# Scores of a gated linear attention by halves of the sequence chunk, in quarters of the TensorE array

## The chip, the cores and the metric

The kernel runs on one core of a Trainium2 chip. The metric is device time in microseconds for one execution, as the median of several runs. Its engines are TensorE (PE in the profile; its weight loads are shown as PEld), VectorE (DVE), ScalarE (ACT), GpSimd (POOL) and SyncE (SP), which only issues transfers here.

## The reference

Two blocks, one after the other. The first is a recurrence per head, with 4 batches, 8 heads, 768 steps and a head size of 48:

```python
state = alpha[:, :, t, :, None] * state + np.einsum('bhd,bhe->bhde', k[:, :, t], v[:, :, t])
y[:, :, t] = np.einsum('bhd,bhde->bhe', q[:, :, t], state)
```

The second takes y as x, 3072 tokens by 384 features (a token's eight heads side by side):

```python
h = x @ w_in            # 384 -> 2048
g = h - np.tanh(h)
return g @ w_out        # 2048 -> 384
```

All is float32.

## The kernel before

**Units and chunks.** A batch's 768 steps are cut into three units of 256 steps (TU), so there are 12 units, numbered u = 0 to 11; a unit has two chunks of 128 steps (c = 0, 1). Inside a chunk the recurrence is a masked product: with U and W, the running products of alpha from both ends (two scans on VectorE, L684 and L700), k is multiplied by U and q by W. Then *scores* (L757) form, for every head, a matrix over s (the step of k and v, 128 partitions) and t (the step of q, 128 columns). *masked* (L767) multiplies it by a triangle, so that s <= t alone is left, on its way from PSUM to the tile pm in SBUF. *products* (L795 and L807) form y: the old state times q, plus v times the masked scores. *back*, *natural* and *update* (L829, L833, L842) carry k times v into the state; *features* (L824) copies y to xT, and *moves* (L885) shifts the rows of the last two heads into gaps by six small transfers, so that the 384 features fill three tiles of 128.

**Heads on the array.** Head size 48 fills less than half of the 128 rows. Heads lie in pairs: four groups g, each with two heads, r = 0 on partitions 0 to 47 and r = 1 on 64 to 111. `head(g, r)` (L527) says which head that is. The two score matmuls of a group use the two row halves of the array; each has 128 weight columns (the steps s) and streams 128 columns (the steps t). Scores of r = 0 and r = 1 lie in one PSUM bank each. The product with the old state (L795) has 48 rows and 64 weight columns, that is one quarter of the array.

**The feed-forward part.** Each unit has eight steps s of `moe` (here a step is 256 of the 2048 features): a first product of 12 matmuls of 128x256 (L951), squares and other functions on ScalarE, products on VectorE (L968, L972, L984 to L986), and a second product, eight matmuls of 128x384 in units 0 and 1 (L996), fourteen of 128x192 from unit 2 on (L1011).

**What sets the order.** All of it is written as tasks (`add`, `go`, `go_c`): a name, an engine, an assumed time in us, a rank, the tasks it comes after, and a function that issues it. `Planner` simulates the engines with these assumed times, in eight rounds with different priorities, and takes the order with the earliest end. The instructions are then issued in that order, and each engine works through its own in order. Waits between engines come from the tiles they share. Transfers are issued on SyncE's queue, all but a few at the start: loads of alpha, k, q (four per unit and tensor, L587), of v (two per unit, L569), weights (L43), moves and stores. v of unit u is loaded once y of unit u - 2 is done, since its buffer has two places.

**Where k, q and alpha come from.** From unit 2 on (and alpha of unit 1) they land as rows of eight steps, get widened on ScalarE (L617) and transposed in 32x32 blocks on VectorE (`flip`, L622). For units 0 and 1 (`TURNED`) they go through TensorE (`turn`, L639).

**PSUM.** The pool ps_sc has two banks, sc0 and sc1. Scores use both; from unit 2 on so do y, and `back` uses sc0.

Of the kernel before, what the change touches and what calls it, by code (L numbers as in the profile page):

```python
# [9 lines left out]
FP32 = mybir.dt.float32  # L10
# [411 lines left out]
def fast(tc, q, k, v, alpha, moe_w_in, moe_w_out, out, w_in, w_out, ident, ok, pad_rows):  # L422
# [17 lines left out]
    with ExitStack() as ctx:  # L440
# [21 lines left out]
        TURNED = ((0, 1, 2), (1, 2))  # L462

        def by_matmul(u, what):
            return u < len(TURNED) and what in TURNED[u]
# [4 lines left out]
        for what in TURNED[0]:  # L470
# [5 lines left out]

        mask = consts.tile([P, P], FP32, name="mask")
        GP.memset(mask, 1.0)
        GP.affine_select(out=mask, in_=mask, compare_op=ALU.is_ge, fill=0.0, base=0,
                         pattern=[[1, P]], channel_multiplier=-1)  # L480

# [37 lines left out]
        def gait(u):  # L519
            return 2  # L520

        plan = Planner()
        add = plan.add
# [3 lines left out]
        def head(g, r):  # L527

            return 2 * g + (r + g) % 2

# [29 lines left out]
        def load(u, what):  # L562

            b, i = divmod(u, UPB)
            t0 = i * TU
            if what == 3:
                vt = vts[u] = two.tile([P, CU, H, D], FP32, name="vt")
                for c in range(CU):
                    (A if u == 0 and c else nc.sync).dma_start(out=vt[:, c],  # L569
                                    in_=v[b, :, t0 + c * P:t0 + (c + 1) * P, :].rearrange("h p d -> p h d"))  # L570
                return
            t, x = raws[what], (alpha, k, q)[what]
            if by_matmul(u, what):
                if u > 0:
                    make_rough(u, what)
                to = rough[u, what][:, 0:BOTH].rearrange("p (h n) -> p h n", h=H)
                of = x[b, :, t0:t0 + TU, :].rearrange("h (p two) d -> p h (two d)", two=CU)

                for n in range(2):
                    at = slice(n * NP, (n + 1) * NP)  # L580
                    (A if u == 0 and n else nc.sync).dma_start(out=to[:, at], in_=of[:, at])  # L581
                return
            for r in range(2):
                a, z = head(0, r), head(1, r)
                src = x[b].rearrange("(e m) s d -> e m (s d)", m=4)[:, a:z + 1:z - a, t0 * D:(t0 + TU) * D]
                for m in range(2):
                    nc.sync.dma_start(out=t[HP * r:HP * r + 32, m::2].rearrange("p e t d -> p e (t d)"),  # L587
                                      in_=src[:, m].rearrange("e (i n) -> i e n", i=32))

        def gla(u, rank):  # L590
# [28 lines left out]
            def flip(what, make):  # L619
                t = make()  # L620
                for g in range(NP):
                    V.transpose(t[:, g].rearrange("p c (i r) -> p r c i", r=R), raws[what][:, g, :, 0:32])  # L622

# [5 lines left out]
            def turn(what, n):  # L629

                if u == 0:
                    pool, tag = ((ps_sc, f"sc{n}"), (ps_o, f"o{n}"), (ps_h, "h"))[what]
                else:
                    pool, tag = ((ps_sc, f"sc{n}"), (ps_o, f"o{2 + n}"), (ps_sc, f"sc{n}"))[what]
                t = m["turned", what, n] = pool.tile([P, NP, P], FP32, name="turned", tag=tag)
                for g in range(NP):
                    for r in range(2):
                        at = (head(g, r) * CU + n) * D
                        T.matmul(t[HP * r:HP * r + HP, g, :], lhsT=rough[u, what][:, at:at + HP], rhs=ident,  # L639
                                 start=True, stop=True)  # L640
# [62 lines left out]
            def scale(name, by):  # L703
                t = m[name].rearrange("p g c t -> p (g c) t")
                V.tensor_mul(t, t, m[by][:, :, 1:])

# [13 lines left out]
            if not by_matmul(u, 1):  # L720
                go("kU", "DVE", 1.2, 3, ["kT", "U"], lambda: scale("kT", "U"))
            if not by_matmul(u, 2):
# [3 lines left out]

            def bank(n, c):


                if u < PLAIN:  # L730
                    return ps_o.tile([P, NP, P], FP32, name="y", tag=f"o{n if c is None else 2 + n}")
                return ps_sc.tile([P, NP, P], FP32, name="y", tag=f"sc{n}")

            def chunk(c):
# [11 lines left out]
                def scores():  # L746
                    if c == 0:

                        xT[u] = two.tile([P, NP, TU], FP32, name="xT")
                    if u == 0 and c == 1:  # L750
                        sc = m["sc", c] = [ps_h.tile([P, 2, TU], FP32, name="h").rearrange(
                            "p a t -> p (a t)").rearrange("p (g t) -> p g t", t=P) for _ in range(2)]
                    else:
                        sc = m["sc", c] = [ps_sc.tile([P, NP, P], FP32, name=f"sc{hh}") for hh in range(2)]
                    for g in range(NP):
                        for r, q in enumerate(quads):
                            T.matmul(sc[r][:, g, :], lhsT=m["kT"][q, g, c, :], rhs=m["qT"][q, g, c, :],  # L757
                                     start=True, stop=True)

                def masked():  # L760
                    if u == 0 and c == 1:
                        pm = [two.tile([P, NP, P], FP32, name=f"pm{hh}", tag=tag) for hh, tag in enumerate("zw")]
                    else:
                        pm = [two.tile([P, NP, P], FP32, name=f"pm{hh}", bufs=1) for hh in range(2)]
                    m["pm", c] = pm
                    for hh in range(2):
                        V.tensor_mul(pm[hh], m["sc", c][hh], mask.unsqueeze(1).to_broadcast([P, NP, P]))  # L767

# [11 lines left out]
                def products():  # L780

                    if n == 0 and direct:
                        one = bank(0, c)
                        m["y", c] = [one, one]
                        y = [one[:, j, :] for j in range(NP)]
                    else:
                        m["y", c] = [bank(x, None if direct else c) for x in range(2)]
                        y = [m["y", c][g % 2][:, g // 2, :] for g in range(NP)]
                    pairs = [(g, r, head(g, r) % 2) for g in range(KT if direct else NP) for r in range(2)]
                    to_gap = [(j, r, hh, slice(HP * hh + D - gap, HP * hh + HP))  # L790
                              for j in range(KT) for r in range(2) for hh in [head(NP - 1, r) % 2]] if direct else []
                    vt = vts[u].rearrange("p c h d -> p c (h d)")
                    if n > 0:
                        for g, r, hh in pairs:
                            T.matmul(y[g][HP * hh:HP * hh + HP], lhsT=old[quads[r], g, :], rhs=m["qT"][quads[r], g, c, :],  # L795
                                     start=(g < 2), stop=False, skip_group_check=True)
                    for j, r, hh, at in to_gap:
# [6 lines left out]
                    for g, r, hh in pairs:  # L804
# [3 lines left out]
                                 rhs=m["pm", c][r][:, g, :],  # L808
                                 start=(n == 0 and g < (1 if direct else 2)), stop=True, skip_group_check=True)

# [4 lines left out]
                def features():  # L815
                    to = slice(c * P, (c + 1) * P)
                    y = m["y", c]
                    if n == 0 and direct:
                        A.copy(xT[u][:, 0:KT, to], y[0][:, 0:KT, :])
                        return  # L820
                    for x in range(2):
                        of = range(x, KT if direct else NP, 2)
                        rows = P if direct else ROWS
                        A.copy(xT[u][0:rows, of.start:of[-1] + 1:2, to], y[x][0:rows, 0:len(of), :])  # L824

                def back():
                    tp = m["tp", c] = bank(0 if u else 1, c)
                    for g in range(NP):
# [6 lines left out]
                def update():  # L835
                    if direct:
                        m["up", c] = bank(1, c).rearrange("p g t -> p (g t)")[:, 0:NP * D]
                    up = m["up", c].rearrange("p (g d) -> p g d", d=D)
# [14 lines left out]
                if past and not (u == 0 and c == 1):  # L853
                    held = [f"masked {past}"]
                    if u > PLAIN or u == PLAIN and c:
                        held += [f"x {past}", not past_last and f"state {past}", not last and "natural"]
                go_c("scores", "PE", 1.2, 7, kU(u) + qW(u) + held, scores)
                go_c("masked", "DVE", 1.4, 8, ["scores", f"y 0.0" if u == 1 and c == 0 else past and u > 0 and f"y {past}"], masked)
                if n > 0:
# [242 lines left out]
        def gather():  # L1102
            verdict["row"] = ps_sc.tile([P, P], FP32, name="row", tag="sc0")
            T.transpose(verdict["row"][0:1, :], verdict["fine"][:, 0:1], ident)
# [74 lines left out]
```

## Time and profile before

| | |
|---|---|
| runs | 600.43, 599.98, 601.09, 597.77 us; median 600.2 |
| the profiled execution | 597.88 us |
| its span, first to last instruction | 595.8 us |
| granted TensorE clock, mean | 0.995 |
| VectorE busy | 438.0 us |
| ScalarE busy | 322.8 us |
| POOL busy | 4.0 us |
| scores, L757 (from SBUF to ps_sc) | 368 matmuls, 285 ns each as shown |
| mask, L767 | 46 instructions of 128x512, 682 ns |
| k times U, L705 | 10 instructions of 128x1024, 1207 ns |
| transposes of k, L622 | 40 of 128x256, 623 ns |
| loads of v, L569 | 192 KB each, 3.6 us from issue to landing |

Durations of matmuls overlap: each shows from its start to the end of its way through the array, and the next starts before that. The cost of a block of matmuls is read from the distance between starts. The span is less than the execution by what lies before the first instruction and after the last. Sixteen further matmuls of scores, of unit 0's second chunk, are shown with another tile's name, because they write to a pool of the feed-forward part.

### The profile page before, as it was taken

What the parts mean: (1) busy time and instruction counts of PE and PEld (TensorE: products, weight loads), DVE (VectorE), ACT (ScalarE), POOL (GpSimd) and SP (SyncE); (2) the same over time, 40 slices, a digit from 0 to 9 for tenths busy, and PEclk for the clock granted to TensorE, in tenths of its full rate; (3) what the DMA queues carried; (4) which work ended last, traced back from release to release, by engine and by line L of the source; (5) the groups of instructions that cost most, each with busy time, mean ns of one, the idle gap of its engine ahead of it and who ended that gap; (6) DMA issues with size and microseconds to landing.
All of it is one profiled execution on the core that took longest, in us unless ns stands there. A gap on an engine that the chain in (4) does not pass through costs nothing.

```text
span 595.8 us, 10679 instructions
## 1 busy us (share of the span) xinstructions
PE 579.8 (97%) x4111; PEld 508.9 (85%) x4111; DVE 438.0 (74%) x830; ACT 322.8 (54%) x585; POOL 4.0 (1%) x18
## 2 busy tenths in 40 slices
PE   8899999999999999999999999999999999999993
PEld 8677777768999998999998999899899898899993
DVE  6968799888979886985896796986796635634742
ACT  3577996448674686576484364264453433423430
POOL 2000000000000000000000000000000000000000
PEclk9999999999999999999999999999999999999997
DMA  9999862245675464452330120220100000000001
GB/s 193 204 238 239 256 125 54 54 113 105 123 144 141 112 161 84 137 133 84 103 113 28 37 57 22 60 80 17 40 6 1 28 8 2 28 8 1 26 1 33
DMA packets 60188, 50.63 MB, mean 85 GB/s; under 512 B 35264, under 2 KB 49888, under 8 KB 60128
## 3 DMA queue, kind: packets, MB, share of 16 engines
q1 hardware_dynamic: 57216, 48.88, 34.9%
q10 hardware_dynamic: 2912, 0.98, 0.8%
q8 instruction: 34, 0.56, 0.4%
q14 instruction: 26, 0.21, 0.1%
HBM read 44.04 MB, written 4.72 MB: 82 GB/s over the span
## 4 chain that ended last, share of the span: by engine, by line
PE 90%; DMA 4%; SPq 2%; DVE 1%; issue 1%; ACT 0%; ACTq 0%; DVEq 0%
PE h L951 42%; PE o L1011 31%; PE o L996 6%; PE sc L757 3%; PE y L807 3%; DMA raw<-in_moe_w_in_dram 2%; PE y L795 2%; DMA vt<-in_v_dram 2%; PE y L842 1%; SPq L43 1%; PE y L829 1%; SPq L569 0%; DVE w_in L87 0%; DMA xT<-xT 0%; ACTq L581 0%
## 5 line engine op out<-in xcount | busy, mean ns | idle before, releaser
L951 PE MATMUL h<-xT,w_in 128*128 128x256 f32 x1152 | 266.1, 381 | 2.7 <-ACT xT L824 1.6
L951 PEld LDWEIGHTS h<-xT,w_in 128*128 128x128 f32 x1152 | 214.8, 190 | 32.3 <-ACT xT L824 1.8
L960 ACT ACTIVATE u<-h 128x512 f32<-128x512 f32 x96 | 57.1, 594 | 191.9 <-PE h L951 191.5
L968 DVE TENSOR_TENSOR w<-h,u 128x512 f32<-128x512 f32 x96 | 65.9, 686 | 89.2 <-ACT u L960 88.9
L1011 PE MATMUL o<-b,e 128*128 128x192 f32 x480 | 91.1, 326 | 0.0
L1011 PE MATMUL o<-w_out,e 128*128 128x192 f32 x320 | 81.2, 336 | 0.0
L1011 PEld LDWEIGHTS o<-b,e 128*128 128x128 f32 x480 | 80.2, 190 | 0.0
L972 DVE SCALAR_TENSOR_TENSOR g<-z,w 128x512 f32<-128x512 f32 x96 | 65.6, 684 | 14.0 <-ACT z L964 10.5
L1011 PE MATMUL o<-b,g 128*128 128x192 f32 x320 | 65.1, 326 | 0.0
L964 ACT ACTIVATE z<-u 128x512 f32<-128x512 f32 x96 | 60.3, 629 | 2.3
L1011 PEld LDWEIGHTS o<-w_out,e 128*128 128x128 f32 x320 | 55.9, 190 | 5.3 <-issue 0.5
L1011 PEld LDWEIGHTS o<-b,g 128*128 128x128 f32 x320 | 54.2, 190 | 0.0
L978 ACT ACTIVATE big<-u 128x1024 f32<-128x1024 f32 x48 | 50.2, 1046 | 0.0
L996 PE MATMUL o<-w_out,g 128*128 128x384 f32 x128 | 44.2, 489 | 0.1
L996 PEld LDWEIGHTS o<-w_out,g 128*128 128x128 f32 x128 | 24.0, 190 | 13.9 <-DVE w_out L87 0.3
L984 DVE TENSOR_TENSOR e<-g 128x256 f32<-128x256 f32 x80 | 33.3, 416 | 1.6
L985 DVE TENSOR_TENSOR e<-g 128x256 f32<-128x256 f32 x80 | 33.3, 416 | 0.0
L767 DVE TENSOR_TENSOR pm<-sc,mask 128x512 f32<-128x512 f32 x46 | 29.5, 682 | 4.9 <-PE sc L757 4.9
L757 PEld LDWEIGHTS sc<-qT,kT 48*128 48x128 f32 x368 | 22.3, 187 | 8.1 <-issue 4.5
L700 DVE TENSOR_TENSOR_SCAN W<-aT,before 128x1032 f32<-128x1032 f32 x12 | 27.6, 2300 | 0.1
L684 DVE TENSOR_TENSOR_SCAN U<-aT,after 128x1032 f32<-128x1032 f32 x12 | 27.4, 2286 | 0.1
L757 PE MATMUL sc<-qT,kT 48*128 48x128 f32 x368 | 26.7, 285 | 0.4 <-DVE rough L469 0.4
(105 smaller groups left out, 534.8 us busy)
## 6 DMA issues: line engine op xcount, KB each, us to landing
raw<-in_moe_w_out_dram SPq DMA_DIRECT2D x16, 768.0 KB, 6.9
raw<-in_moe_w_in_dram SPq DMA_DIRECT2D x32, 288.0 KB, 5.8
vt<-in_v_dram SPq DMA_DIRECT2D x23, 192.0 KB, 3.6
ar<-in_alpha_dram SPq DMA_DIRECT2D x44, 96.0 KB, 2.3
kr<-in_k_dram SPq DMA_DIRECT2D x40, 96.0 KB, 2.2
qr<-in_q_dram SPq DMA_DIRECT2D x40, 96.0 KB, 2.2
raw<-in_moe_w_in_dram SPq DMA_DIRECT2D x32, 96.0 KB, 5.9
out_dram<-same SPq DMA_DIRECT2D x20, 96.0 KB, 1.7
```

The lines of the kernel that those rows point to most:

```text
L757: T.matmul(sc[r][:, g, :], lhsT=m["kT"][q, g, c, :], rhs=m["qT"][q, g, c, :], start=True, stop=True)
L767: V.tensor_mul(pm[hh], m["sc", c][hh], mask.unsqueeze(1).to_broadcast([P, NP, P]))
L951: T.matmul(h[:, a, :], lhsT=w_in[:, j, f * P:(f + 1) * P], rhs=xT[u][:, j, :], start=(j == 0), stop=(j == KT - 1))
L960: A.activation(m["u", s], m["h", s], AF.Square, scale=W_SCALE ** -1.5)
L964: A.activation(m["z", s], m["u", s], AF.Square, bias=QB, scale=QA * W_SCALE)
L968: V.tensor_mul(m["w", s], m["h", s], m["u", s])
L972: V.scalar_tensor_tensor(out=g.rearrange("p a c t -> p (a c t)"), in0=m["z", s], scalar=QK, in1=m["w", s], op0=ALU.add, op1=ALU.mult)
L978: A.activation(big, m["us", s // 2].rearrange("p s t -> p (s t)"), AF.Relu, bias=-U_FAST, scale=W_SCALE, accum_out=over[:, n:n + 1])
L984: V.tensor_add(e[:, 0:2, :], g[:, 0], g[:, 1])
L985: V.tensor_sub(e[:, 2:4, :], g[:, :, 1, :], g[:, :, 0, :])
L996: T.matmul(m["o"][c], lhsT=g[:, a, c, :], rhs=w_out[:, f, :], start=(f == 0), stop=(f == FT - 1))
L1011: T.matmul(o[n][:, i], lhsT=g_, rhs=w_, start=(s == 0 and (n, i) in ((0, 0), (1, 0), (2, 1), (3, 0))), stop=(s == FS - 1), skip_group_chec ...
```

## The change

For units 2 to 11 (`halved`), three things go together.

*Scores.* Instead of one matmul of 128 weight columns per head, there are two of 64 weight columns. The first takes the first half of s and streams all 128 steps t; the second takes the second half of s and streams only the second half of t, since for s in the second half and t in the first the mask is zero anyway. The steps s of heads 4 to 7 (groups 2 and 3) are swapped by halves: what is the first half of s for them lies on the upper 64 partitions. So groups 0 and 2 fill the two column halves of the array at the same time, with the two heads of each in the two row halves, and matmuls are ordered by groups 0, 2, 1, 3.

*What follows from the swap.* v of heads 4 to 7 is loaded with its halves exchanged: per chunk one transfer for heads 0 to 3 and two of 64 rows for heads 4 to 7, so six per unit instead of two. The transpose of k writes groups 2 and 3 in swapped order, and its product with U becomes two instructions. The heads are placed on groups in another way (`head`), so that groups 0 and 1 hold heads 0 to 3, and the loads are grouped accordingly.

*Mask.* It is now one tile with four groups' triangles, set by three selections on GpSimd. pm is one lasting tile, whose quarters that are never written are zeroed once, at unit 2, on GpSimd. Masking is three instructions: the second half of t on all partitions for all heads, and the first half of t on 64 partitions for groups 0 and 1 and for groups 2 and 3.

Besides, for all units: scores use one tile of two banks (`two_banks`), y's groups lie in banks by g // 2 instead of g % 2, and from unit 2 on `features` is one copy of both banks instead of two. The planner's assumed times are new for three tasks of the halved units: scores 1.0 (1.2), masked 1.55 (1.4), k times U 1.4 (1.2).

```diff
+        def halved(u):
+            return u >= len(TURNED)
...
-            return 2 * g + (r + g) % 2
+            return 2 * g + (r + (g >= NP // 2)) % 2
...
+                    of = v[b, :, t0 + c * P:t0 + (c + 1) * P, :].rearrange("h p d -> p h d")
+                    if not halved(u):
+                        (A if u == 0 and c else nc.sync).dma_start(out=vt[:, c], in_=of)
+                        continue
+                    nc.sync.dma_start(out=vt[:, c, 0:NP], in_=of[:, 0:NP])
+                    for x in range(2):
+                        nc.sync.dma_start(out=vt[HP * x:HP * x + HP, c, NP:],
+                                          in_=of[HP - HP * x:P - HP * x, NP:])
...
-                    V.transpose(t[:, g].rearrange("p c (i r) -> p r c i", r=R), raws[what][:, g, :, 0:32])
+                    to = t[:, g].rearrange("p c (i r) -> p r c i", r=R)
+                    if what == 1 and halved(u) and g >= NP // 2:
+                        to = to.rearrange("p r c (x i) -> p r c x i", x=2)[:, :, :, ::-1, :]
+                    V.transpose(to, raws[what][:, g, :, 0:32])
...
+                    for half in range(2):
+                        for g in (0, 2, 1, 3):
+                            rows = HP * (half ^ (g >= NP // 2))
+                            for r, q in enumerate(quads):
+                                T.matmul(sc[r][rows:rows + HP, g, HP * half:], lhsT=m["kT"][q, g, c, rows:rows + HP],
+                                         rhs=m["qT"][q, g, c, HP * half:], start=True, stop=True)
...
+                    if u == len(TURNED) and c == 0:
+                        GP.memset(pm[HP:P, :, 0:NP // 2, 0:HP], 0.0)
+                        GP.memset(pm[0:HP, :, NP // 2:, 0:HP], 0.0)
+                    for rows, gs, ts in ((slice(0, P), slice(0, NP), slice(HP, P)), (slice(0, HP), slice(0, NP // 2), slice(0, HP)),
+                                         (slice(HP, P), slice(NP // 2, NP), slice(0, HP))):
+                        to, of = (x[rows, :, gs, ts] for x in (pm, sc))
+                        V.tensor_mul(to, of, mask[rows, gs, ts].unsqueeze(1).to_broadcast(list(to.shape)))
...
+                    if u >= PLAIN:
+                        both = m["y", c][2]
+                        A.copy(xT[u][0:ROWS, :, to].rearrange("p (a b) t -> p a b t", a=2), both[0:ROWS, :, 0:2, :])
+                        return
...
-                go_c("scores", "PE", 1.2, 7, kU(u) + qW(u) + held, scores)
+                go_c("scores", "PE", 1.0 if halved(u) else 1.2, 7, kU(u) + qW(u) + held, scores)
```

## The prediction

> **What bounds the kernel now.** I read the page's busy times first, then the chain that ended last, then TensorE's timeline inside one unit, then the queue of SyncE where a transfer stands on the chain.
>
> ```profile
> span 595.8 us, 10679 instructions
> PE 579.8 (97%) x4111; PEld 508.9 (85%) x4111; DVE 438.0 (74%) x830; ACT 322.8 (54%) x585; POOL 4.0 (1%) x18
> PE 90%; DMA 4%; SPq 2%; DVE 1%; issue 1%; ACT 0%; ACTq 0%; DVEq 0%
> ```
>
> TensorE is busy 97% of the span and is 90% of the chain. A busy PE need not be at its peak, so I looked for gaps: from 150 to 500 us the sums by stretch give PE busy all of every stretch, and DVE 79.2 of 100 us between 200 and 300. There, what TensorE no longer has to do comes off the time, while VectorE and ScalarE have room. Before 150 us it is otherwise (VectorE 26.8 of 30 us from 120 to 150).
>
> The timeline of TensorE and of its weight loads in one unit (start, length, engine, line):
>
> ```profile
> 280.81 1.16 PE L757 MATMUL sc<-qT,kT 48*128 48x128 f32 x16
> 286.97 0.67 PE L795 MATMUL y<-qT,state 48*64 48x128 f32 x16
> 288.48 0.62 PE L842 MATMUL y<-vt,kn 128*48 128x48 f32 x16
> ```
> ```profile
> 280.81 0.97 PEld L757 LDWEIGHTS sc<-qT,kT 48*128 48x128 f32 x16 [0.33 <-ACT big L978]
> 281.90 0.30 PEld L1011 LDWEIGHTS o<-w_out,e 128*128 128x128 f32 x2
> ```
>
> A block of work costs TensorE the distance from its first weight load to the next block's. Scores (L757) take 281.90 - 280.81 = **1.09 us** per chunk. Line 795 has the shape that the changed scores take, 48 rows by 64 weight columns, 128 columns streamed: 16 matmuls in 287.56 - 286.97 = 0.59 us.
>
> **The sum, part by part.**
>
> *Scores of heads by halves.* Followed one instruction at a time, the old block runs in pairs (two row halves of the array): the second pair starts 213 ns after the first, each further one 112 ns later, and the next block's load 200 ns after the last start: 213 + 6 x 112 + 7 + 200 = 1092 ns. Line 795 runs four at a time, one per quarter of the array: starts 7 ns apart within a four, the second four 160 ns after the first, further ones each 109 ns later, and 198 ns from last start to the next block. The new block has 16 matmuls of 128 columns (four fours at 109) and 16 of 64 columns (four more fours). No row shows a four of 64 columns. Nearest is line 842, where one column half loads 64 weight columns and streams 48: eight matmuls are 0.62 us less one of 0.222, over seven steps = 57 ns. Streaming 64 of 128 columns is half of 107, so also about 54 plus the same few ns. Bounds: 54 ns, if only streaming counts, to 109, if a four of half length costs as much as a full one. I take 58. Block: 160 + 3 x 109 + 4 x 58 for the starts less one step (the first short four starts at 160 + 2 x 109 + 109 = 487, the last at 661), 20 within the last four, and 54 + 91 of exit (198 less the 107 of streaming = 91) = **826 ns**. It saves 266 ns in each of 20 chunks (units 2 to 11, two each): **5.3 us**. At 109 throughout the block would be 160 + 6 x 109 + 20 + 145 = 979: 2.3 us. Units 0 and 1 keep their form.
>
> A rule speaks against the small pieces. The Trainium skill, "TensorE: Matmul & The Clock Gate", section "Wait — 56ns, not 53.3ns?", says that starts of matmuls never come closer than about 25 ns however small they are. Counted over the whole array, four would take 100 ns, and the block 160 + 3 x 109 + 3 x 100 + 75 + 145 = 1007 ns, a saving of 1.7 us in all. But the row has starts 7 ns apart in line 795, and 16 in 0.59 us with its entry and exit: the floor is not one across quarters here. I sum by the row.
>
> *The mask.*
>
> ```profile
> L767 DVE TENSOR_TENSOR pm<-sc,mask 128x512 f32<-128x512 f32 x46 | 29.5, 682 | 4.9 <-PE sc L757 4.9
> L705 DVE TENSOR_TENSOR kT<-kT,U 128x1024 f32<-128x1024 f32 x10 | 12.1, 1207 | 0.0
> L984 DVE TENSOR_TENSOR e<-g 128x256 f32<-128x256 f32 x80 | 33.3, 416 | 1.6
> L824 ACT COPY xT<-y 112x256 f32<-112x256 f32 x44 | 15.1, 370 | 16.1 <-PE y L807 12.7 <-PE y L842 2.4 <-DVE state L850 1.0
> L833 ACT COPY kn<-y 128x448 f32<-128x448 f32 x20 | 10.4, 522 | 7.5 <-PE y L829 7.4
> ```
>
> Two of 682 ns become one of 512 elements (682) and two of 256 on half the partitions (416 each, by line 984): +0.15 us x 20 = 3.0 us of VectorE. *k times U* becomes two of 512 (682): +0.16 x 10 = 1.6. The transpose into swapped halves moves as many elements; 625 ns before, I take no change (no row has this write order; double for half of the 40 would be 12.5 us of VectorE, spread over 450 us). These hide behind TensorE, which does a first product or a second product (2.2 to 2.8 us each) between scores and y. If the cover were gone, 0.15 us per chunk, 3.0 us in all, would reach TensorE. In the stage from 90 to 150 us the addition is 4 x 0.15 + 2 x 0.16 = 0.9 us against 6.3 us of VectorE's idle time.
>
> *Copies of y.* Two of 370 become one of 512 columns: 370 + (522 - 370) / 192 x 256 = 573 ns, 0.17 less, but it waits for line 842 also in its first half. x is complete about 0.2 us later; the transfers behind it stand 13 us or more ahead of their use from unit 3 on. One tile for both banks of scores adds no wait that the planner's order doesn't already have (back after x and state).
>
> *Start.* On POOL, the mask's memset grows from 128 to 512 elements (206 to about 540 ns by 428 for 384), and one selection becomes three of twice the width; ident, behind the memset, comes about 0.3 us later, the zeroed rows of the scans 1.3 us later (needed at 8.29, ready at 3.6). The 0.3 reaches the first turns on TensorE, but the chain then waits for weights of the second part (1.1 us of waiting in the products at 34.6): taken as 0, at most 0.3. Two memsets of pm on POOL at unit 2 (316 ns each by its row of 256) find POOL idle and their readers gone for 40 us: 0.
>
> *SyncE's queue.* Loads of v go from 2 transfers to 6 per unit: 40 more in all. This is the part with a price. Behind SyncE's issues stand the moves of x and the loads of alpha, k and q.
>
> ```profile
> 123.60 1.15 SPq L569 DMA_DIRECT2D vt<-in_v_dram  x2
> 124.84 3.95 SPq L885 DMA_DIRECT2D xT<-xT  x6
> 126.94 1.78 DMA xT<-xT
> 128.86 3.16 PE h L951 x12
> ```
>
> The first two lines are SyncE's timeline, the others the chain. Unit 4's v is issued just ahead of unit 2's moves, and unit 2's first product waits for the fourth move. Its waits are already 0.5 us before and 0.3 inside the product. An issue of alpha, k or q, of similar shape, takes 0.42 us with 0.05 between: six take 2.8 instead of 1.24, so the moves start **1.6 us** later, and TensorE waits that much more. Bounds: four more at 0.58 are 2.5 us; if the moves come ahead, the present 0.8 is gained. I take 1.6. Elsewhere it is hidden: unit 3's moves end at 161.7 and are used at 173.4; later units have 13 us or more; and the eight more issues at 74.7 us (v of units 2 and 3, 8 x 0.47 = 3.8 us) delay the alpha of unit 3 from a landing at about 79.6 + 2.3 = 81.9 to 85.7. Its copy on ScalarE began at 84.35, so it begins 1.3 us later. Queued behind it are a z, a sum over u and the next product's square at 88.86, which itself waited 0.37 for TensorE: it comes 0.9 late, and its reader on VectorE stands 2.2 us after its end (89.46, 91.71). So nothing of it reaches TensorE; without that gap it would be 0.9.
>
> *Sum:* -5.3 + 1.6 = **-3.7 us**. The profiled execution was 597.88 us, 2.1 outside the span; it becomes 594.2. It lies 0.4% below the median of 600.2, which becomes **596.5**. A difference under 0.5%, 3 us, can hardly be told from none here.
>
> **The rivals.**
>
> (1) *The queue costs nothing*: the planner gets new times for scores (1.0), masked and k times U, and may put the moves first. For it: it searches with these times. Against: v is ready when y is, a copy before x. 600.2 - 5.3 - 0.8 = 594.1 at best.
>
> (2) *The short fours don't pay*: a four of 64 columns takes as long as one of 128. Nothing in the profile runs it. -2.3 + 1.6 gives 599.5: no change that can be measured. Against it are the 57 ns of line 842.
>
> (3) *Slower.* The new times make another order of everything, and one queue, VectorE's in the stage of 60 to 150 us, puts the chain of a unit (scan of U, transposes, scan of W: 2.3 + 2.05 + 2.3 + 2.05 us) behind work that isn't urgent. PE then has no product ready, since unit 2 waits for its x. One such chain late, 8.7 us, gives 596.5 + 8.7 = 605.2; it decides from 3.7 + 3.0 = 6.7 us of new waits. For it: VectorE is at 88% there. Against: the added work is 0.9 us, and TensorE waits under 1 us there now.
>
> **How the numbers follow.** Forecast 0.48 (594.8 to 598.0), rival 1 0.22, rival 2 0.16, rival 3 0.14. Faster by over 0.5% (below 597.2): 0.38 of the forecast, nearly all of rival 1 (0.21), a little of rival 2 (0.01) = 0.60. Slower (above 603.2): rival 3 less its mild part, 0.11. Within: 0.29. The range 593.4 to 602.6 leaves about 0.11 of rival 3 above and 0.06 below.
>
> **What would show it.** Scores as 640 matmuls of 48 by 64, and from their first load to the next block 0.83 us (0.98: rival 2; 1.0: the floor). VectorE about 4.6 us busier, ScalarE 3.3 less. Unit 2's first product waiting for a move, with six issues of v ahead. TensorE without a gap from 150 us on. The prediction is wrong if a wait of several us appears for VectorE or SyncE before 150 us, or if the order changes how often TensorE switches its form.

## The result, and the profile after

The changed kernel takes 596.4 us in the median (41 runs), the kernel before 599.65 (62 runs). The ratio is 0.9939, with a 95% interval of 0.9925 to 0.9953, that is 3.7 us less (2.8 to 4.5). It compares means, which lie further apart than the medians, and leaves out one execution of the changed kernel (601.9 us) that fell in the chip's slower state. The forecast was 596.5, 3.7 us less than the 600.2 it started from. The number is right; two of the terms behind it are not, their errors nearly cancel, and the experiments below say which.

One pair of executions would not have shown it. The profiled execution of before, 597.88 us, is among its faster ones, that of after, 596.37, is at its median, and single executions range from 596.8 to 603.4 before and from 591.7 to 600.3 after. In the two traces, unit 11's first product starts (first weight load) at 542.55 and at 542.57 us: what was saved by then has been given back. Of that, 2.1 us are lost before unit 1's first product (77.84 us against 75.73), in the stage in which the weights arrive, and 2.8 us between the first products of units 3 and 5. The 1.2 us between the spans lie in the last stores. So the traces say what each block and each wait costs, and the medians say what is gained.

The page of the changed kernel, and its groups of matmuls and of VectorE and ScalarE by shape:

```profile
span 594.6 us, 11389 instructions
PE 575.1 (97%) x4431; PEld 504.5 (85%) x4431; DVE 443.1 (75%) x860; ACT 322.0 (54%) x565; POOL 5.8 (1%) x22
PE 72%; DMA 13%; ACT 4%; SPq 4%; DVE 3%; issue 2%; ACTq 0%; DVEq 0%
...
L796 PE MATMUL sc<-qT,kT 48*64 48x128 f32 x320 | 13.3, 282 | 2.6 <-ACT kn L888 2.5
L796 PE MATMUL sc<-qT,kT 48*64 48x64 f32 x320 | 8.2, 218 | 0.0
...
L818 DVE TENSOR_TENSOR pm<-sc,mask 64x256 f32<-64x256 f32 x40 | 16.7, 417 | 0.3
L818 DVE TENSOR_TENSOR pm<-sc,mask 128x512 f32<-128x512 f32 x20 | 13.7, 685 | 3.1 <-PE sc L796 3.0
L874 ACT COPY xT<-sc 112x512 f32<-112x512 f32 x20 | 11.6, 582 | 15.3 <-PE sc L897 11.0 <-PE sc L858 3.6 <-DVE state L905 0.7
```

VectorE is 5.1 us busier. TensorE, 90% of the chain before, is 72% now, and DMA has gone from 4% to 13%. That is the first sign that something other than TensorE has come onto the path that ended last.

TensorE and its weight loads in one unit of the changed kernel (start, length):

```profile
283.54 0.90 PE L796 MATMUL sc<-qT,kT 48*64 48x128 f32 x32
...
283.54 0.76 PEld L796 LDWEIGHTS sc<-qT,kT 48*64 48x64 f32 x32 [0.33 <-ACT big L1033]
284.37 0.30 PEld L1066 LDWEIGHTS o<-w_out,e 128*128 128x128 f32 x2
```

A block of scores, from its first weight load to the next block's, is 284.37 - 283.54 = 0.83 us; followed one instruction at a time it is 828 ns in all 20 chunks (1092 before). With 20 x 0.264 = 5.3 us less to do, TensorE should have ended 5.3 us earlier. What its weight loads waited for after 180 us (at 186.6, 218.6, 265.9 and 403.5 us) stands in two lines (sum, number of waits, longest):

```profile
PEld sc L796 <- ACT kn L888: 3.8, 3, 2.1
...
PEld sc L884 <- DVE state L905: 1.4, 1, 1.4
```

Before, the second wait does not occur, and of the first there is one of 0.3 us:

```profile
PEld sc L757 <- ACT kn L833: 0.3, 1, 0.3
```

The longest ends at 265.85 us, where the weight loads of scores had waited 2.1 us (their matmuls 1.7) for kn on ScalarE. Here is ScalarE, and then SyncE's queue, on the way there, in the changed kernel:

```profile
254.70 0.62 ACT L633 COPY ar<-ar 32x512 f32<-32x512 f32 x1 [4.24 <-DMA ar<-in_alpha_dram]
...
260.60 1.26 ACT L633 COPY kr<-kr 32x512 f32<-32x512 f32 x2 [2.18 <-DMA kr<-in_k_dram]
...
265.28 0.51 ACT L888 COPY kn<-sc 128x448 f32<-128x448 f32 x1
```
```profile
244.14 0.39 SPq L584 DMA_DIRECT2D vt<-in_v_dram  x1
244.58 1.27 SPq L586 DMA_DIRECT2D vt<-in_v_dram  x2
245.89 0.60 SPq L584 DMA_DIRECT2D vt<-in_v_dram  x1
246.54 1.26 SPq L586 DMA_DIRECT2D vt<-in_v_dram  x2
247.90 3.73 SPq L940 DMA_DIRECT2D xT<-xT  x6
251.73 1.94 SPq L603 DMA_DIRECT2D ar<-in_alpha_dram  x4
```

And SyncE's queue at the same place before:

```profile
242.91 1.01 SPq L569 DMA_DIRECT2D vt<-in_v_dram  x2
243.97 4.08 SPq L885 DMA_DIRECT2D xT<-xT  x6
248.15 1.94 SPq L587 DMA_DIRECT2D ar<-in_alpha_dram  x4
```

Loading v takes 3.7 us of the queue where it took 1.0, and alpha leaves at 251.73 where it left at 248.15 (v itself was also issued 1.2 us later). ScalarE works in order: it stands still for alpha, then for k, and the copy of kn, which has nothing to do with either and whose product was done at 261.6, comes behind them. TensorE was 2.7 us later than before when it began unit 5 (268.90 against 266.17, first weight loads).

Near unit 2's first product, where the forecast had put its price, SyncE's queue in the changed kernel reads:

```profile
123.77 3.74 SPq L940 DMA_DIRECT2D xT<-xT  x6
127.61 0.53 SPq L584 DMA_DIRECT2D vt<-in_v_dram  x1
```

The moves stand ahead of v here. The new assumed times made another order, and unit 2's product doesn't wait for a move at all. What the 2.1 us before unit 1's first product come from stays open; the kernel with v in two (below), in the same order, is 1.4 us behind there too, and the one with the new order alone 0.6.

### The profile page after: what moved, and what is told of

It reads as the page before. It is cut to its first block, busy times and chain, and to the rows that moved or that the text cites. A ratio compares the mean times of both kernels' runs of the same rounds, so it can differ in the third digit from the quotient of the medians.

```text
span 594.6 us, 11389 instructions
## 1 busy us (share of the span) xinstructions
PE 575.1 (97%) x4431; PEld 504.5 (85%) x4431; DVE 443.1 (75%) x860; ACT 322.0 (54%) x565; POOL 5.8 (1%) x22
## 4 chain that ended last, share of the span: by engine, by line
PE 72%; DMA 13%; ACT 4%; SPq 4%; DVE 3%; issue 2%; ACTq 0%; DVEq 0%
PE h L1006 33%; PE o L1066 25%; PE o L1051 6%; DMA raw<-in_moe_w_in_dram 5%; PE sc L858 3%; DMA ar<-in_alpha_dram 3%; PE sc L796 3%; DMA vt<-in_v_dram 2%; PE sc L846 2%; DMA kr<-in_k_dram 1%; DMA raw<-in_moe_w_out_dram 1%; SPq L940 1%; PE sc L897 1%; DMA qr<-in_q_dram 1%; SPq L603 1%
## 5 line engine op out<-in xcount | busy, mean ns | idle before, releaser
L818 DVE TENSOR_TENSOR pm<-sc,mask 64x256 f32<-64x256 f32 (+1 forms) x60 | 28.7, 506 | 3.3 <-PE sc L796 3.0
L83 ACT ACTIVATE more<-raw 128x768 int16<-128x768 uint32 x16 | 17.2, 1077 | 14.6 <-DMA raw<-in_moe_w_in_dram 12.1
L796 PEld LDWEIGHTS sc<-qT,kT 48*64 48x64 f32 x640 | 15.2, 133 | 10.0 <-issue 4.6
```

The costliest lines, as they stand in the source:

```text
L796: T.matmul(sc[r][rows:rows + HP, g, HP * half:], lhsT=m["kT"][q, g, c, rows:rows + HP], rhs=m["qT"][q, g, c, HP * half:], start=True, stop ...
L818: V.tensor_mul(to, of, mask[rows, gs, ts].unsqueeze(1).to_broadcast(list(to.shape)))
```

## Experiments

Two theories for what was given back. *SyncE*: six issues of v per unit hold up alpha and k behind them. *Order*: the planner's new order makes the waits, and v is hidden. ("In six" and "in two" are the transfers per unit.) The first four kernels take the three parts (scores in quarters, v in six, new order) in different sets. Ratios are to the kernel before, on the same chip.

**v in two.** In the changed kernel:

```diff
-                    if not halved(u):
+                    if True:
                         (A if u == 0 and c else nc.sync).dma_start(out=vt[:, c], in_=of)
```

> The changed kernel, with v of units 2 to 11 loaded by two transfers per unit instead of six, as in the kernel before; the halves of s of heads 4 to 7 are then not swapped in v, so that these heads' y is left wrong. Order and everything else are those of the changed kernel. Theory 'SyncE': the six issues of v (3.9 us in the changed kernel's trace, 1.2 before) push the loads of alpha and k behind them back, and the waits of scores for kn and of back for state, 3 to 5 us in all after 180 us, come from that. Then this kernel has nearly the whole of TensorE's 5.3 us: ratio to before 0.991 (594.3 us or less), and no wait over 0.5 us on TensorE from 150 us on. Rival 'order': the planner's new order makes the waits; then it stays where the changed kernel is, 0.994, with the same waits.

0.9878 (0.9848 to 0.9909), 591.6 us. The waits of scores for kn shrink to one, and that of *natural* (L884) for state is gone:

```profile
PEld sc L796 <- ACT kn L888: 0.8, 1, 0.8
```

This is *SyncE*. The gain is even more than the 5.3 us: 7.3 (5.5 to 9.1).

**Old times.** In the changed kernel:

```diff
-                go("kU", "DVE", 1.4 if halved(u) else 1.2, ...
+                go("kU", "DVE", 1.2, ...
-                go_c("scores", "PE", 1.0 if halved(u) else 1.2, ...
+                go_c("scores", "PE", 1.2, ...
-                go_c("masked", "DVE", 1.55 if halved(u) else 1.4, ...
+                go_c("masked", "DVE", 1.4, ...
```

> The changed kernel with the planner's assumed times of before (scores 1.2, masked 1.4, k times U 1.2), so that all tasks come in the order of the kernel before. Theory 'SyncE': v of unit 4 stands again ahead of unit 2's moves, so unit 2's first product waits some 2 us more, and alpha stays late in later units: ratio 0.993 to 0.997. Rival 'order': the waits of the new order are gone, ratio 0.991.

1.0027 (1.0003 to 1.0051), 601.0 us: slower than either theory said. In the order of before, the change would have lost a little. TensorE waits 3.1 us for a move at unit 2, and at 223.8 and 270.7 us for kn again.

**The kernel before with the new times** (the same three edits the other way):

> The kernel before with the three assumed times of the changed kernel (from unit 2 on), so that it has the changed kernel's order and nothing else of the change. Theory 'SyncE': the order alone costs nothing, ratio 0.998 to 1.002. Rival 'order': the order costs 1.5 us or more, ratio 1.003 to 1.006.

0.9980 (0.9955 to 1.0005): 1.2 us less, with an interval from 2.7 less to 0.3 more. The order alone costs nothing like the 1.5 us or more of that theory. *Order* falls.

**The kernel before with v in six:**

```diff
+                    of = v[b, :, t0 + c * P:t0 + (c + 1) * P, :].rearrange("h p d -> p h d")
+                    if u < len(TURNED):
+                        (A if u == 0 and c else nc.sync).dma_start(out=vt[:, c], in_=of)
+                        continue
+                    nc.sync.dma_start(out=vt[:, c, 0:NP], in_=of[:, 0:NP])
+                    for x in range(2):
+                        nc.sync.dma_start(out=vt[HP * x:HP * x + HP, c, NP:],
+                                          in_=of[HP * x:HP * x + HP, NP:])
```

> The kernel before, in its own order, with v of units 2 to 11 loaded by six transfers per unit (same data, not swapped). Theory 'SyncE', and the prediction's step on the moves: unit 2's first product waits 2 to 2.8 us more, and alpha's loads come later in every unit: ratio 1.003 to 1.007. Rival 'order': the transfers are hidden, ratio 0.999 to 1.001.

1.0129 (1.0101 to 1.0157), 7.7 us: above the largest value that any theory gave. Here the mechanism of the forecast is on show, in the order that it assumed. SyncE's queue, and then TensorE, in this kernel:

```profile
123.45 0.41 SPq L573 DMA_DIRECT2D vt<-in_v_dram  x1
123.91 1.27 SPq L575 DMA_DIRECT2D vt<-in_v_dram  x2
125.22 0.61 SPq L573 DMA_DIRECT2D vt<-in_v_dram  x1
125.88 1.26 SPq L575 DMA_DIRECT2D vt<-in_v_dram  x2
127.24 3.73 SPq L891 DMA_DIRECT2D xT<-xT  x6
```
```profile
127.08 1.16 PE L763 MATMUL sc<-qT,kT 48*128 48x128 f32 x16
131.08 4.51 PE L957 MATMUL h<-xT,w_in 128*128 128x256 f32 x12 [2.84 <-DMA xT<-xT]
135.44 1.78 PE L1002 MATMUL o<-w_out,g 128*128 128x384 f32 x5
```

The product starts 2.2 us later than before (131.08 against 128.86), and then takes 4.51 us where it took 3.16 before: 1.35 more. The table by stretch of the same kernel says why (its columns: stretch, its length, busy time of PE, PEld, DVE, ACT and POOL, then the granted clock, DMA share, GB/s):

```profile
128.00:131.00 3.00, 0.24 (x6) 0.05 (x2) 3.00 (x4) 0.00 (x0) 0.00 (x0) 1.00 0.18 37
131.00:134.00 3.00, 2.92 (x7) 2.34 (x8) 0.53 (x1) 0.00 (x0) 0.00 (x0) 0.52 0.45 129
134.00:137.00 3.00, 3.00 (x11) 2.11 (x11) 0.73 (x2) 1.31 (x3) 0.00 (x0) 0.91 0.99 201
...
219.88:223.29 3.41, 1.84 (x21) 1.29 (x19) 3.41 (x6) 3.38 (x9) 0.00 (x0) 1.00 0.07 12
223.29:226.70 3.41, 3.41 (x11) 3.41 (x12) 3.41 (x9) 2.80 (x6) 0.00 (x0) 0.50 0.78 217
```

After nearly 3 us without work the clock is 0.52 in the next 3 us. The last two rows show the same further on: scores wait 1.57 us for kn until 222.1, and from 223.29 on the clock is half for 3.41 us, 1.2 us after work had begun again. TensorE is 3.3 us later there. Unit 2's wait with its clock makes 3.6, this 3.3, unit 5 another 1.4; that is all but 0.1 of the 8.4 by which unit 11 starts later in the trace.

So six issues cost 1.29% here (against before), 1.2% in the changed kernel with the old order (1.0027 less the 0.9909 of "v in two, old times" below) and 0.6% with the new one. The new order with v in six and the old scores was not run.

Eight more kernels: the size of the parts, and where v could go instead.

**The second half of s streams all 128 steps.** In the changed kernel:

```diff
-                                T.matmul(sc[r][rows:rows + HP, g, HP * half:], lhsT=...
-                                         rhs=m["qT"][q, g, c, HP * half:], start=True, stop=True)
+                                T.matmul(sc[r][rows:rows + HP, g, :], lhsT=...
+                                         rhs=m["qT"][q, g, c, :], start=True, stop=True)
```

> The changed kernel with the second half of s streaming all 128 steps t too (16 more matmuls of 128 columns in place of 64; the extra quarter is masked out by being ignored). It measures what the short fours are worth. If streaming sets the time of a four, as the prediction took it (58 against 109 ns), the block of scores takes 4 x 51 ns more, 0.83 -> 1.03 to 1.04 us, 4.1 us over 20 chunks: ratio to before 1.000 to 1.002. If a short four cost as much as a long one, the block stays at 0.83 us (already excluded by the trace for the block, not for the time).

1.000 (0.998 to 1.002); the block of scores takes 1034 ns:

```profile
285.71 0.86 PEld L796 LDWEIGHTS sc<-qT,kT 48*64 48x64 f32 x32 [0.33 <-ACT big L1033]
286.74 0.30 PEld L1066 LDWEIGHTS o<-w_out,e 128*128 128x128 f32 x2 [0.17 <-issue]
```

A four of 64 columns is thus (1034 - 828) / 4 = 51 ns shorter than one of 128, close to half of the 107 ns that the prediction took for streaming 128. Without leaving out the quarter, and with v in six on SyncE, the whole change would be worth nothing.

**v in two, old times.** Both edits above.

> The changed kernel with v in two transfers per unit (heads 4 to 7 left wrong, since their v isn't swapped) and the planner's assumed times of before: the scores, masks and copies of the change in the order of before, without the six issues. By the prediction's step on scores the ratio is 1 - 5.3/599.5 = 0.991 (0.990 to 0.992). If the change to scores, masks and copies carries a cost or a gain of its own besides TensorE's 5.3 us, it differs by that.

0.9909 (0.9885 to 0.9933), 5.5 us less (4.0 to 6.9), in the order of before: the scores' 5.3 us fit, and masks and copies cost nothing that can be seen.

**Half-height loads on GpSimd's queue.** In the changed kernel:

```diff
-                        nc.sync.dma_start(out=vt[HP * x:HP * x + HP, c, NP:],
+                        GP.dma_start(out=vt[HP * x:HP * x + HP, c, NP:],
```

> The changed kernel with the four half-height loads of v per unit issued from GpSimd's queue, which is idle, so that SyncE has two issues of v per unit as before. Data and result are those of the changed kernel. Theory 'SyncE's issue time': ratio to before 0.986 to 0.990, as with v in two (0.988), and no wait of scores for kn over 0.5 us. Rival 'more transfers': if it is not the issue time but the transfers themselves that delay alpha and k, it stays near 0.994.

0.9903 (0.9875 to 0.9930), 594.2 us, just outside what was expected. Its interval leaves out the rival's 0.994, but just overlaps that of the changed kernel (0.9925 to 0.9953). The traces decide it: from unit 1's first product to unit 11's it takes 461.6 us, with v in two 461.3, the changed kernel 464.9. The waits for kn are 1.0 us in one place. The transfers are all still there, so their data was not the cost; their place in SyncE's queue was. What is missing lies before: unit 1's first product comes at 79.46 us, with v in two at 77.10. The loads on GpSimd's queue leave early here too (see below), and the clock is half from 50.03 to 53.44 us.

**The planner told what v costs.** In the changed kernel:

```diff
-                go(f"load {name}", "SP", 1.3 if direct or ... else 2.0, ...
+                go(f"load {name}", "SP", 3.9 if what == 3 and halved(u) else 1.3 if direct or ... else 2.0, ...
```

> The changed kernel with the planner's assumed time for a load of v of units 2 to 11 at 3.9 us (2.0), which is what six issues take in the trace. Theory 'the planner doesn't know': with the true price it puts these loads where nothing urgent stands behind, ratio 0.988 to 0.991. Rival: the queue is too full for any place, or other assumed times are off by as much, and it stays at 0.993 to 0.997.

0.9905 (0.9876 to 0.9933), 594.1 us. One number in the plan is worth about as much as another queue. Its interval, too, just overlaps that of the changed kernel.

**All of v on GpSimd's queue**, without and with the planner told that SyncE has 0.1 us left to do for it. The half-height loads as above, and besides:

```diff
-                    nc.sync.dma_start(out=vt[:, c, 0:NP], in_=of[:, 0:NP])
+                    GP.dma_start(out=vt[:, c, 0:NP], in_=of[:, 0:NP])
```

> The changed kernel with all six loads of v per unit (units 2 to 11) on GpSimd's queue, so that SyncE issues none of them. Data and result are those of the changed kernel. Theory 'SyncE's issue time': at or a little below the kernel with four of six there: ratio to before 0.985 to 0.990, and alpha's landing no later than before. If GpSimd's own issue is too slow for v, or disturbs VectorE, it is worse than 0.990.

> The same, and the planner told that a load of v of units 2 to 11 takes 0.1 us of SyncE instead of 2.0, which is now so. If the planner's picture of SyncE's queue matters as it did for the price of 3.9, the order gets better: ratio 0.984 to 0.988. If the order is as good as it gets already, it is the same as without, within 0.3%.

0.9953 (0.9923 to 0.9983) and 0.9933 (0.9904 to 0.9961): against the expectation, no better than the changed kernel, and by the middle values worse than four of six there. From unit 1's first product on, the traces have no such loss: up to unit 11's they take 460.9 us each, with v in two 461.3. It lies before (unit 1's first product at 81.57 and 82.78 us), in a wait that the changed kernel's trace has once, with 0.3 us (it varies: the kernel that streams all 128 steps has one of 1.6). TensorE's waits and GpSimd's timeline in the first of the two:

```profile
PEld o L1051 <- DVE w_out L87: 3.9, 2, 2.1
```
```profile
25.90 0.89 POOL L584 DMA_DIRECT2D vt<-in_v_dram  x1 [20.09 <-ACT xT L879]
26.78 1.24 POOL L586 DMA_DIRECT2D vt<-in_v_dram  x2
```

v of units 2 and 3 used to stand behind other work in SyncE's queue and left at 77 to 84 us. On an empty queue it leaves at 26 and 61 us, as soon as its buffer is free, while the DMA engines are full (share 1.04 to 1.24 from 10 to 70 us) with the weights. The weights are late then, and the clock is half for 3.41 us from 45.12 us (in the second kernel for 6.83 from 43.98). That v's early loads do this is so far only read from the trace. The next two kernels test it:

**v on GpSimd's queue from unit 4 on**, without and with prices (3.9 for units 2 and 3, 0.1 for later ones):

```diff
+                    (GP if u > 3 else nc.sync).dma_start(out=vt[:, c, 0:NP], in_=of[:, 0:NP])
...
+                        (GP if u > 3 else nc.sync).dma_start(out=vt[HP * x:HP * x + HP, c, NP:],
```

> The changed kernel with v of units 4 to 11 on GpSimd's queue (all six issues), and v of units 2 and 3 on SyncE's as in the changed kernel. Theory 'too early': with all of v on GpSimd, v of units 2 and 3 left at 26 and 61 us instead of 76, into the 70 us in which the DMA engines are full with the weights, and weights came late; kept on SyncE's queue they come after the weights again. Then the ratio to before is 0.985 to 0.989, and TensorE doesn't wait over 0.5 us from 80 us on. Rival 'GpSimd's queue itself disturbs': it stays at 0.993 or more.

> The same with the planner told 3.9 us of SyncE for v of units 2 and 3 and 0.1 for later units. If true prices make a better order, 0.983 to 0.987; if the order is settled by other things, within 0.3% of the kernel without.

0.9873 (0.9843 to 0.9904) and 0.9857 (0.9828 to 0.9887), 593.2 and 591.8 us. The first differs from all-on-GpSimd (0.9953) only in the queue, and so the time, of the loads of two units; its waits for w_out are back to one of 0.3 us. Both beat the changed kernel; which of the two is better can't be told. TensorE by stretch in the second (columns as above):

```profile
90.00:150.00 60.00, 60.00 (x452) 45.37 (x451) 55.51 (x87) 37.42 (x68) 4.11 (x6) 1.00 0.31 82
150.00:300.00 150.00, 150.00 (x1197) 136.33 (x1196) 126.39 (x253) 101.50 (x188) 15.78 (x24) 1.00 0.53 127
300.00:500.00 200.00, 200.00 (x1597) 181.67 (x1595) 148.33 (x303) 93.06 (x165) 11.85 (x18) 1.00 0.13 35
```

It is without a gap from 90 us on; what waits are left lie in the stage of the weights.

## Why the prediction was right, and where it was not

- **Scores, -5.3 us: right.** 826 ns forecast, 828 in the trace; with v in two and the old order 5.5 us in measured time. The price of a short four (58 ns, from line 842) was right, and the floor of 25 ns between starts does not hold across quarters: 7 ns there too.
- **Masks, k times U, transposes, copies: right.** 685 + 2 x 417 = 1519 ns for a mask (1514 forecast), 665 + 684 for k times U, 624 for a transpose as before, 582 for the copy of y (573). None shows as a cost: -5.5 was measured with all of them in, which by its interval leaves room for at most 1.3 us. ScalarE's busy time fell by 0.8 us, not by the 3.3 forecast; the durations of its instructions, added up without regard to overlap, fell by 3.2.
- **The start: about right.** The spin's wait for ident grew from 1.5 to 1.9 us (0.3 forecast).
- **SyncE's queue: the step that failed.** That issues of v hold up what stands behind them was right, but three things were wrong. *Place:* the moves of unit 2 went first in the new order, which the prediction had as rival 1's premise; the wait that its 1.6 us stand for does not occur. *Cover:* "Elsewhere it is hidden" looked at the moves' slack and at one alpha in the early stage, not at alpha and k in later units, which stand behind v and on whose landing ScalarE stops in order. So its sign "without a gap from 150 us on" failed, and the waits came after 180 us, not before 150 where it looked for them. *Size:* six issues took 3.7 us, not 2.8 (its upper bound, 2.5 more than the 1.24, is what came), and in the old order waits also cost clock afterwards. v in six costs 0.61% here (0.9939 less 0.9878, 3.7 us) and 1.3% in the old order, where 1.6 us had been summed.
- **The order: counted as nothing.** With v in two, the new order is at 0.9878 and the old at 0.9909, a gain of 1.9 us, though the intervals overlap and 1.2 was measured for the order alone. The traces show where: unit 2's first product no longer waits for moves (0.8 us, rival 1's term), and from the last matmul to the end it takes 8.2 us after and 8.1 with v in two, against 9.4 before and 8.8 in the old order with v in two. So 3.7 comes out as 5.5 + 1.9 - 3.7, where the forecast had 5.3 - 1.6: two errors of about 2 us in opposite directions. That the sum was met to 0.1 us is luck.
- **Rival 1** (queue costs nothing) is wrong about the cost, right about the moves going first. **Rival 2** (short fours don't pay) is wrong. **Rival 3** (a slower order): the order itself wasn't slower; the slower outcome existed, but on SyncE's queue, with the old order (1.0027).

## What to carry to other kernels

A change that splits a transfer is priced by what stands behind it in the issuing queue: list each load there, and on which engine, working in order, the next one waits for it. If a plan is made from assumed times, a task that grew has to be given its new time; one number, 2.0 to 3.9, was worth about 2 us here (0.9905 against 0.9939, with intervals that just overlap). An empty queue isn't free either: what was held back by a full one starts earlier, and can delay what is needed first (0.9953 against 0.9873 here).

## What the runs showed of the hardware that was not expected

- A short wait of TensorE can cost more than its length. After 2.8 us without a matmul a product took 4.51 us instead of 3.16; a wait of 1.57 us made TensorE 3.3 us later. In all fourteen traces the granted clock, once up, fell only to 0.50 before TensorE's work ended, for 3.41 us (once for 6.83), and always a whole number of such stretches after the trace's first clock record. The stretch before held 1.57 to 2.84 us without a matmul. No stretch at full clock with less was followed by a fall, and six with 1.67 to 1.95 us were not either. How a wait lies on the stretches thus matters: that of 1.7 us before 265.85 in the changed kernel is cut in two at 265.27 and was followed by a clock of 1.00. The Trainium skill, "TensorE: Matmul & The Clock Gate", Part 1, has a half-rate clock after an idle window of about 3.4 us that runs freely. Rate and length agree with the 0.50 and 3.41 us here; but stretches that were idle for 46 to 83% of their length were enough, and where exactly the limit lies no run here settles.
- An issue of 48 KB of v on SyncE takes no less than one of 192 KB: 0.62 and 0.52 us in the median, and 0.57 for 96 KB. From GpSimd's queue it takes 0.62 (0.76 for the loads of 96 KB). So between 48 and 192 KB the number of issues counted, not their size.
- Four matmuls of 48x64 in the four quarters of the array run side by side, one four each 109 ns for 128 columns and each 58 for 64, with starts 7 ns apart within a four.
